# An attention block's backward stage: middle part reordered, side work given more yields and another step rate, dK stored from ScalarE one head later

## The chip, the cores and the metric

One core of one Trainium2 chip. The metric is device time in microseconds (us) of one launch. The kernel was already tuned: 1750 us in the median, with most runs within 0.4% of that. A ratio in this document is the mean time of one kernel's fast runs over that of the kernel before in the same rounds, with a 95% interval; so it is not quite the ratio of the two medians that stand beside it. "0.9942" means 0.58% faster, about 10 us; 0.1% is 1.75 us.

## The reference

A decoder block for one new token of each of 4 sequences: attention over a cache (32 heads, 4096 keys, head size 128), then a gated MLP, both after a layernorm, and the gradients of all inputs and weights.

```python
q = (layernorm(x) @ wq)                      # 4 x 32 heads x 128
p = softmax(q k^T / sqrt(128));  o = p v     # 4 x 32 heads over 4096 keys
h = x + o @ wo
out = h + (silu(lnh @ w1) * (lnh @ w3)) @ w2
out, vjp = jax.vjp(f, x, k_cache, v_cache, wq, wo, w1, w3, w2)   # out and 8 gradients
```

The caches make the weight of it: K and V are 128 heads of 1 MB each. The forward reads both; the backward stage reads V once more (dP = dO V^T) and writes dK and dV, 128 MB each. All else that is moved comes to 34 MB.

## The kernel before

All big tiles live in 22 buffers of 1 MB, handed out in a ring: a buffer that is given back goes to the end of the line, and who takes it next has to wait until the last transfer or instruction on it is over.

```python
free = deque(range(NSLOT))                 # 22 buffers
class Slot:
    def __init__(self, name): self.i = free.popleft(); ...
    def give(self):           free.append(self.i)
```

The backward stage goes head by head. `front` transposes V on TensorE (copies by ScalarE) and makes dP; `back` makes dV and dK as outer products on VectorE and stores both from GpSimd's queue. SyncE loads V up to seven heads ahead. Beside it runs a generator of "side work" (dq, dx and the weight gradients), cut by `yield` into about 200 steps, of which each head takes one, two or three.

```python
def grad_unit(dst, lhsT, rhs):             # one 128 x 512 piece of a weight gradient
    ...
    nc.tensor.matmul(ps[:, 0:n], lhsT=lhsT, rhs=rhs, start=True, stop=True)
    nc.scalar.copy(out=dst, in_=ps[:, 0:n])

def back(s):
    ...
    gv = Slot("gv"); outer(gv.heads(), P2, reps["rdo", s // REP][:, s % REP, :])
    nc.gpsimd.dma_start(out=rows_of(out_3[b, h]), in_=gv.heads()); gv.give()
    ...
    gk = Slot("gk"); outer(gk.heads(), dS2, reps["rq", s // REP][:, s % REP, :])
    nc.gpsimd.dma_start(out=rows_of(out_2[b, h]), in_=gk.heads()); gk.give()

def prefetch(s):
    while nv["next"] < min(NH, s + 7) and len(free) > 5:
        load_V2()                          # from SyncE

for s in range(NH):                        # NH = 128
    prefetch(s + 1)
    ...
    if s + 1 < NH: front(s + 1)
    back(s)
    step("s", 1 if s < 42 else 2 + s % 2)  # side work
step("s", 400)
```

Between forward and backward lies "the joint": the attention output times wo, the MLP and its backward for four rows, a serial chain whose weights hold most of the buffers.

## Time and profile before

The prediction below sizes the stages (the full forward, the joint, the full backward stage with a hole at 1160 us, the last stores) and shows the lines for it. Two views that it does not show are needed later. The first is the list of transfers by kind (count, KB each, median us from issue to landing); the second a table of windows of the second half (the last three columns: granted clock, DMA share, GB/s).

```profile
V<-in_A_v_cache_dram SPq DMA_DIRECT2D x128, 1024.0 KB, 11.1
out_dram<-gv POOLq DMA_DIRECT2D x128, 1024.0 KB, 19.6
out_dram<-gk POOLq DMA_DIRECT2D x128, 1024.0 KB, 19.6
```

### The profile page before, as it was taken

To read this page: it belongs to the slowest core of one execution; us is meant where nothing else is said; L and a number is where in the kernel's file an instruction comes from. 1 tells how busy PE (TensorE), PEld (TensorE's weight loads), DVE (VectorE), ACT (ScalarE), POOL (GpSimd) and SP (SyncE) were. 2 spreads that over 40 slices of the span, in tenths; PEclk is the share of its full clock that TensorE was granted. 3 is DMA by queue.
4 is the path that set the end of the run, shared out by engine and by line. 5 is a ranking of instruction groups with operands and counts; after the bars stand their busy time and mean duration, and the time that the engine had idled before them with its cause. 6 is when DMAs were issued, how large, how long until landed. Compare 5 with 4: busy or idle time off the path is not lost.

```text
span 1747.4 us, 44078 instructions
## 1 busy us (share of the span) xinstructions
PE 1324.0 (76%) x18993; PEld 1120.0 (64%) x18993; DVE 1254.4 (72%) x1385; ACT 953.7 (55%) x1460; POOL 487.4 (28%) x805
## 2 busy tenths in 40 slices
PE   5889888888888887878877886676787777476574
PEld 4667666677666666778766875555555556365563
DVE  5989899889998995557756757565465667475585
ACT  3455445445444544555554555675666667475463
POOL 2333333333333330112421333222222123132132
PEclk8999999999999999655555556765565556565555
DMA  9999999999999998699999999999999999999997
GB/s 398 410 418 418 419 418 419 418 412 418 418 415 398 418 407 313 257 422 421 410 414 418 415 416 413 422 383 426 417 418 416 414 412 406 422 407 410 424 417 303
DMA packets 107123, 707.86 MB, mean 405 GB/s; under 512 B 11232, under 2 KB 18920, under 8 KB 23984
## 3 DMA queue, kind: packets, MB, share of 16 engines
q1 hardware_dynamic: 67280, 422.68, 59.1%
q0 software_dynamic: 39648, 282.36, 39.2%
q8 instruction: 149, 2.44, 0.5%
q14 instruction: 46, 0.38, 0.1%
HBM read 422.58 MB, written 282.34 MB: 403 GB/s over the span
## 4 chain that ended last, share of the span: by engine, by line
DMA 38%; DVE 11%; issue 6%; PE 4%; ACT 3%; POOL 1%; DVEq 0%; POOLq 0%; ACTq 0%; SPq 0%
DMA out_dram<-gk 22%; DMA out_dram<-gv 12%; DVE gk L1053 4%; DVE gv L1053 4%; DMA V<-in_A_v_cache_dram 2%; ACT VT L740 2%; PE pt_tps L739 1%; DMA out_dram<-gw 1%; POOL P L1049 1%; DMA w<-in_B_w_dram 1%; DVE PK L421 1%; DVE dS L1071 0%; PE M_ps L436 0%; DVE dSt L1068 0%; PE o_ps L961 0%
## 5 line engine op out<-in xcount | busy, mean ns | idle before, releaser
L740 ACT COPY VT<-pt_tps 128x1024 bf16<-128x1024 bf16 x512 | 492.4, 1016 | 250.7 <-PE pt_tps L739 122.8
L739 PE MATMUL pt_tps<-ident_b,V 128*128 128x128 bf16 x4096 | 458.2, 296 | 147.0 <-ACT VT L740 147.0
L739 PEld LDWEIGHTS <-V 128*128 128x128 bf16 x4096 | 408.1, 140 | 211.6 <-issue 202.1
L1053 DVE TENSOR_TENSOR gv<-P,reps 128x4096 bf16<-128x4096 bf16 x128 | 292.9, 2288 | 234.0 <-DMA out_dram<-gk 141.1
L1053 DVE TENSOR_TENSOR gk<-dS,reps 128x4096 bf16<-128x4096 bf16 x128 | 293.4, 2292 | 67.0 <-DMA out_dram<-gv 29.7
L421 DVE TENSOR_TENSOR PK<-Kn,PK 128x4096 bf16<-128x4096 bf16 x128 | 302.9, 2366 | 35.9 <-POOL PK L417 35.9
L436 PE MATMUL M_ps<-PK,Vn 128*128 128x130 bf16 x4096 | 285.9, 222 | 47.0 <-DMA Vn<-in_A_v_cache_dram 46.1
L436 PEld LDWEIGHTS <-Vn 128*128 128x128 bf16 x4096 | 253.0, 99 | 67.3 <-DMA Vn<-in_A_v_cache_dram 61.0
L328 DVE STREAM_TRANSPOSE KT<-Kn 128x512 f32<-128x512 f32 (+1 forms) x321 | 250.9, 798 | 0.5 <-issue 0.5
L323 ACT COPY KT<-pt_tps 128x1024 bf16<-128x1024 bf16 x128 | 129.4, 1012 | 188.0 <-PE pt_tps L322 155.8
L1046 PE MATMUL dP_ps<-dOT_bf,VT 128*128 128x1 bf16 x4096 | 152.6, 166 | 66.0 <-ACT VT L740 65.3
L1046 PEld LDWEIGHTS <-VT 128*128 128x128 bf16 x4096 | 141.3, 104 | 78.1 <-ACT VT L740 77.6
L1075 POOL DMA_DIRECT2D out_dram<-gk x128 | 68.2, 533 | 384.3 <-DVE gk L1053 377.1
L1065 POOL DMA_DIRECT2D out_dram<-gv x128 | 68.4, 535 | 347.6 <-DVE dSt L1068 333.5
L417 POOL COPY PK<-P_all 128x64 bf16<-128x64 bf16 x128 | 32.3, 253 | 436.9 <-ACT P_all L411 424.6
L336 POOL COPY zq<-qT_bf 128x2 bf16<-128x2 bf16 x128 | 152.2, 1189 | 0.0
L1049 POOL COPY P<-P_all 128x64 bf16<-128x64 bf16 x128 | 117.4, 918 | 0.0
L411 ACT COPY P_all<-pt_P 32x64 bf16<-32x64 bf16 x256 | 51.9, 203 | 58.2 <-PE pt_P L407 56.0
L322 PE MATMUL pt_tps<-ident_b,Kn 128*128 128x128 bf16 x1024 | 80.6, 223 | 0.7 <-DVE qrep L282 0.7
L446 PE MATMUL kP_ps<-PK,onesw 128*32 128x512 bf16 x1024 | 79.2, 386 | 0.0
L322 PEld LDWEIGHTS <-Kn 128*128 128x128 bf16 x1024 | 62.1, 100 | 26.5 <-issue 26.5
L400 ACT ACTIVATE Pn<-E,rl 128x1024 bf16<-128x1024 f32 x64 | 73.7, 1151 | 2.8 <-DVE rl L397 2.8
(221 smaller groups left out, 1288.3 us busy)
## 6 DMA issues: line engine op xcount, KB each, us to landing
Kn<-in_A_k_cache_dram SPq DMA_DIRECT2D x128, 1024.0 KB, 14.9
Vn<-in_A_v_cache_dram SPq DMA_DIRECT2D x128, 1024.0 KB, 14.7
V<-in_A_v_cache_dram SPq DMA_DIRECT2D x128, 1024.0 KB, 11.1
out_dram<-gv POOLq DMA_DIRECT2D x128, 1024.0 KB, 19.6
out_dram<-gk POOLq DMA_DIRECT2D x128, 1024.0 KB, 19.6
wq<-in_A_wq_dram SPq DMA_DIRECT2D x8, 1024.0 KB, 14.6
out_dram<-gw POOLq DMA_DIRECT2D x6, 896.0 KB, 21.7
wo<-in_A_wo_dram SPq DMA_DIRECT2D x4, 1024.0 KB, 14.5
```

What stands on the lines that cost most here:

```text
L322: nc.tensor.transpose(pt[:, i, :], Kn[:, c * GW + i, :], ident_b[:])
L323: nc.scalar.copy(out=KT[:, c * GW:(c + 1) * GW, :], in_=pt[:])
L328: nc.vector.transpose(out=KT[:, c * w_:(c + n) * w_], in_=Kn[:, c * w_:(c + n) * w_])
L336: nc.gpsimd.tensor_copy(out=zq[gi % 2][hl][:, 32:132:67], in_=qT_bf[:, s:s + 1].to_broadcast([P, 2]))
L421: nc.vector.tensor_tensor(out=PK[:, :, 0:Dh].rearrange("p j (r t) -> p j r t", t=2), in0=Ks[s].heads().rearrange("p j (r t) -> p j r t", t=2),
L436: nc.tensor.matmul(hold["M"][:], lhsT=Vn[:, j, :], rhs=PK[:, j, :], start=(j == 0), stop=(j == SJ - 1))
L446: nc.tensor.matmul(hold["kP"][32 * q:32 * (q + 1), :, :], lhsT=ones_window(w), rhs=PK[:, j0:j0 + 4, 0:Dh], start=(w == 0 and c == 0), stop ...
L739: nc.tensor.transpose(pt[:, i, :], Vn[:, g * GW + i, :], ident_b[:])
L740: nc.scalar.copy(out=VT[:, g * GW:(g + 1) * GW, :], in_=pt[:])
L1046: nc.tensor.matmul(dP_ps[:, j:j + 1], lhsT=VT[:, j, :], rhs=dOT_bf[:, s:s + 1], start=True, stop=True)
L1049: nc.gpsimd.tensor_copy(out=P2[:], in_=P_all[:, s, :, None].to_broadcast([P, SJ, 2]))
L1053: nc.vector.tensor_tensor(out=dst.rearrange("p j (r t) -> p j r t", t=2), in0=col2[:, :, None, :].to_broadcast([P, SJ, Dh // 2, 2]), in1=r ...
```

## The change

Its intent: shorten the joint, so that buffers come free and V loads start sooner; take the waits out of the side work by more yields and by copying a gradient unit only when the next one is under way; take the dK stores off GpSimd's queue, so that three engines issue instead of two. No byte more or less moves. The core of the diff (the reordering of the joint, some 80 lines, is cut to two lines and a comment; the comments are ours):

```diff
+            # joint: w1/w3 transposes before the attention pages, wo transposes spread over the
+            # gaps, layernorm applied after the transposes, the first two V transposes no longer there
-        V_T(0, psT)
+        woT(5, "ssvsv")
...
         def grad_unit(dst, lhsT, rhs):
...
-            nc.scalar.copy(out=dst, in_=ps[:, 0:n])
+            grad_flush()                    # copy of the unit before
+            gu.append((dst, ps, n))
...
             wqT.give()
+            yield                           # eight yields more, this one ahead of dx's reader
             fs = Slot("fin")
...
             outer(gk.heads(), dS2, reps["rq", s // REP][:, s % REP, :])
-            nc.gpsimd.dma_start(out=rows_of(out_2[b, h]), in_=gk.heads())
+            late.append((b, h, gk))
+
+        def store_gk():
+            b, h, gk = late.popleft()
+            nc.scalar.dma_start(out=rows_of(out_2[b, h]), in_=gk.heads())
             gk.give()
...
                 front(s + 1)
+            if late:
+                store_gk()
             back(s)
-            step("s", 1 if s < 42 else 2 + s % 2)
+            step("s", 1 if s < 44 else 2 + (s % 4 == 0))
+        store_gk()
         step("s", 400)
```

More of the change, by code (lines that the diff above doesn't have):

```diff
@@ L476, in attn_page @@
         if pg == 0 or last:
-            hold["at"] = psX.tile([P, 512], FP32, tag="x", name="at_ps")
+            hold["at"] = psK.tile([P, 512], FP32, tag="kP", name="al_ps") if last else psX.tile([P, 512], FP32, tag="x", name="at_ps")
         at_ps = hold["at"]
         for k in range(8):
-            c = 0 if last else k % 4
+            c = 0 if last else k % 2
             nc.tensor.matmul(at_ps[32 * c:32 * c + B, :], lhsT=OT_bf[:, (8 * pg + k) * B:(8 * pg + k + 1) * B],
                              rhs=wo_page(8 * pg)[:, k].rearrange("p c n -> p (c n)"),
-                             start=(k == 0 if last else pg == 0 and k < 4), stop=(k == 7 if last else pg == H // 8 - 2 and k >= 4),
+                             start=(k == 0 if last else pg == 0 and k < 2), stop=(k == 7 if last else pg == H // 8 - 2 and k >= 6),
                              tile_position=(0, 32 * c))
         if pg >= H // 8 - 2:
-            for c in range(1 if last else 4):
+            for c in range(1 if last else 2):
                 nc.vector.tensor_tensor(out=hrows[:], in0=hrows[:], in1=at_ps[32 * c:32 * c + B, :], op=ALU.add)
@@ L578 @@
     pending = deque()
-    for nm, ap in (("w1", B_w1), ("w3", B_w3)):
+    for nm, ap in (("w3", B_w3), ("w1", B_w1)):
         for i in range(2):
@@ L693 @@
     weights(NGI)
-    w13T(4, "sv")
     M_mm(NH - 2, 0, SJ)
@@ L697 @@
     weights(NGI)
-    w13T(4, "sv")
     M_mm(NH - 1, 0, SJ)
@@ L702 @@
     O_cols(NH - MC, NH)
+    kP_flush(NH - 1)
     w13T(len(tunits), "sv")
-    kP_flush(NH - 1)
     for pg in range(H // 8 - 1):
         attn_page(pg)
-        woT(4, "sv")
+        if pg > 0:
+            woT(1, "s")
     attn_page(H // 8 - 1)
@@ L756 @@
         psT = cm.enter_context(tc.tile_pool(name="psTm2", bufs=4, space=bass.MemoryType.PSUM))
-        hs = Slot("hhat")
-        hhat = hs.f(D)[0:B, :]
         while free:
             load_V2()
-        layernorm_rows(hrows[:], B, hhat, rstd_h[:])
-        nc.scalar.activation(out=warm[:], in_=warm[:], func=AF.Exp)
-        woT(len(wo_units), "s")
+        pt = psA.tile([P, DC, B], FP32, tag="rT", name="pt_hT")
+        for c in range(DC):
+            nc.tensor.transpose(pt[:, c, :], hrows[0:B, c * P:(c + 1) * P], ident_f[0:B, 0:B])
@@ new lines @@
+        stats = small.tile([B, 1, nc.vector.BN_STATS_DIM], FP32, tag="ln_stats", name="ln_stats")
+        nc.vector.bn_stats(out=stats[:, 0, :], in_=hrows[:])
+        mv = small.tile([B, nc.vector.BN_AGGR_DIM], FP32, tag="ln_mv", name="ln_mv")
+        nc.vector.bn_aggr(out=mv[:], in_=stats[:])
+        nc.vector.tensor_scalar(out=rstd_h[:], in0=mv[:, 1:2], scalar1=eps, scalar2=None, op0=ALU.add)
+        woT(1, "s")
+        nc.scalar.sqrt(rstd_h[:], rstd_h[:])
+        nc.scalar.activation(out=warm[:], in_=warm[:], func=AF.Exp)
@@ new lines @@
+        woT(2, "s")
+        rdiag = mid.tile([B, 2 * B], FP32, name="rdiag")
+        nc.vector.tensor_scalar(out=rdiag[:, 0:B], in0=ident_f[0:B, 0:B], scalar1=mv[:, 0:1], scalar2=None, op0=ALU.mult)
+        nc.vector.reciprocal(out=rstd_h[:], in_=rstd_h[:])
+        nc.vector.tensor_scalar(out=rdiag[:, B:2 * B], in0=ident_f[0:B, 0:B], scalar1=rstd_h[:], scalar2=None, op0=ALU.mult)
+        rb_ps = psA.tile([P, 2 * B], FP32, tag="rT", name="rb_ps")
+        nc.tensor.matmul(rb_ps[:], lhsT=ones_f[0:B, :], rhs=rdiag[:], start=True, stop=True)
@@ L764 @@
+        woT(1, "s")
+        rb = mid.tile([P, 2 * B], FP32, name="rb")
+        nc.vector.tensor_copy(out=rb[:], in_=rb_ps[:])
         hhatT = mid.tile([P, DC, B], BF16, name="hhatT")
         hhatT_f = mid.tile([P, DC, B], FP32, name="hhatT_f")
-        pt = psA.tile([P, DC, B], FP32, tag="rT", name="pt_hT")
-        for c in range(DC):
-            nc.tensor.transpose(pt[:, c, :], hhat[:, c * P:(c + 1) * P], ident_f[0:B, 0:B])
-        nc.vector.tensor_copy(out=hhatT[:], in_=pt[:])
-        nc.vector.tensor_copy(out=hhatT_f[:], in_=pt[:])
@@ L771 @@
-        nc.gpsimd.tensor_copy(out=hhat_bf[:], in_=hhat)
-        hs.give()
-        while free:
-            load_V2()
+        nc.vector.tensor_tensor(out=hhatT_f[:], in0=pt[:], in1=rb[:, None, 0:B].to_broadcast([P, DC, B]), op=ALU.subtract)
+        nc.vector.tensor_tensor(out=hhatT[:], in0=hhatT_f[:], in1=rb[:, None, B:2 * B].to_broadcast([P, DC, B]), op=ALU.mult)
+        nc.vector.tensor_tensor(out=hhatT_f[:], in0=hhatT_f[:], in1=rb[:, None, B:2 * B].to_broadcast([P, DC, B]), op=ALU.mult)
@@ L775 @@
+        nc.vector.tensor_scalar(out=hhat_bf[:], in0=hrows[:], scalar1=mv[:, 0:1], scalar2=rstd_h[:],
+                                op0=ALU.subtract, op1=ALU.mult)
         w1, w3 = mid_w["w1"], mid_w["w3"]
@@ L783 @@
             sl.give()
-        while len(free) > 1:
+        while free:
             load_V2()
-        rdiag = mid.tile([B, B], FP32, name="rdiag")
-        nc.vector.tensor_scalar(out=rdiag[:], in0=ident_f[0:B, 0:B], scalar1=rstd_h[:], scalar2=None, op0=ALU.mult)
-        rb_ps = psA.tile([P, B], FP32, tag="rT", name="rb_ps")
-        nc.tensor.matmul(rb_ps[:], lhsT=ones_f[0:B, :], rhs=rdiag[:], start=True, stop=True)
-        rb = mid.tile([P, B], FP32, name="rb")
-        nc.vector.tensor_copy(out=rb[:], in_=rb_ps[:])
         gateT = mid.tile([P, FC, B], FP32, name="gateT")
@@ L821 @@
             sl.give()
-        while len(free) > 1:
+        while free:
             load_V2()
-        V_T(1, psT)
+        woT(len(wo_units), "s")
         z = mid.tile([P, 2, DC, B], FP32, name="z")
@@ L841 @@
                                        in1=u[:], op0=ALU.mult, op1=ALU.add)
-        nc.vector.tensor_tensor(out=u[:], in0=u[:], in1=rb[:, None, :].to_broadcast([P, DC, B]), op=ALU.mult)
+        nc.vector.tensor_tensor(out=u[:], in0=u[:], in1=rb[:, None, B:2 * B].to_broadcast([P, DC, B]), op=ALU.mult)
         nc.vector.tensor_tensor(out=dhT[:], in0=u[:], in1=grT[:], op=ALU.add)
@@ L876, with grad_flush @@
         bw3 = c2.enter_context(tc.tile_pool(name="bw3", bufs=3, reuse_waits="tile"))
+        gu = []
+        def grad_flush():
+            if gu:
+                dst, ps, n = gu.pop()
+                nc.scalar.copy(out=dst, in_=ps[:, 0:n])
         def grad_unit(dst, lhsT, rhs):
@@ L899, in side_work @@
             flat = Slot("dqflat")
+            yield
             for b in range(B):
@@ L928, in side_work @@
                             nc.tensor.transpose(pt[:, i, cc, :], wv[:, cc, (hl + i) * Dh:(hl + i + 1) * Dh], ident_b[:])
+                    yield
                     nc.scalar.copy(out=wqT.b(HH * D).rearrange("p (n c) -> p n c", c=P)[:, hl * DC:(hl + 2) * DC, :],
                                    in_=pt.rearrange("p a c k -> p (a c) k"))
-                    yield
                 wq2.give()
+                yield
                 for hl in range(HH):
@@ L938, in side_work @@
             wqT.give()
+            yield
             fs = Slot("fin")
@@ L954, in side_work @@
                     yield
+                grad_flush()
                 nc.gpsimd.dma_start(out=out_4[cc * P:(cc + 1) * P, :], in_=st.b(HD))
@@ L963, in side_work @@
                 sl.give()
+            yield
             h2_bf = rs.t[0:B, 2560:2560 + D]
@@ L974, in side_work @@
                         nc.tensor.transpose(pt[:, c, :], srcT[:, c0 + c, :], ident_b[:])
+                    yield
                     nc.scalar.copy(out=dst_rows[:, c0 * P:(c0 + 7) * P].rearrange("b (c f) -> b c f", f=P), in_=pt[:])
-                    yield
             for i in range(2):
@@ L982, in side_work @@
                     yield
+                grad_flush()
                 nc.gpsimd.dma_start(out=out_8[i * 7 * P:(i + 1) * 7 * P, :].rearrange("(c p) j -> p c j", p=P),
@@ L993, in side_work @@
                             yield
+                    grad_flush()
                     nc.gpsimd.dma_start(out=out_ap[i * 2 * P:(i + 1) * 2 * P, :].rearrange("(c p) f -> p c f", p=P),
@@ L1012, in side_work @@
                     yield
+                grad_flush()
                 nc.gpsimd.dma_start(out=out_5[h0 * P:(h0 + 8) * P, :].rearrange("(h p) j -> p h j", p=P),
@@ L1074, in back @@
             outer(gk.heads(), dS2, reps["rq", s // REP][:, s % REP, :])
-            nc.gpsimd.dma_start(out=rows_of(out_2[b, h]), in_=gk.heads())
+            late.append((b, h, gk))
+        late = deque()
+        def store_gk():
+            b, h, gk = late.popleft()
+            nc.scalar.dma_start(out=rows_of(out_2[b, h]), in_=gk.heads())
             gk.give()
```

## The prediction

> **What bounds the kernel now.** I read the page's slices first, then a table of windows by stage, then the chain of work that ended last between 690 and 730 us, and the longest waits.
>
> The first fence is the page's second part, 40 slices of 43.7 us each.
>
> ```profile
> PEclk8999999999999999655555556765565556565555
> DMA  9999999999999998699999999999999999999997
> GB/s 398 410 418 418 419 418 419 418 412 418 418 415 398 418 407 313 257 422 421 410 414 418 415 416 413 422 383 426 417 418 416 414 412 406 422 407 410 424 417 303
> ```
>
> The DMA row is full nearly everywhere: no engine sets the pace, the 16 transfer engines do. Only four places fall below: slices 15 and 16 (313, 257 GB/s), slice 26 (383) and the last (303). The page gives 422.58 MB read and 282.34 MB written, and the change moves no byte more or less; at the 424 GB/s that full 5 us windows reach, these 704.9 MB take 1663 us. So time can come only from the holes and from the rate in full stretches. The table of windows (columns: length, busy us and count of PE, PEld, DVE, ACT, POOL, then clock, DMA share, GB/s) sizes the stages:
>
> ```profile
> 0.00:660.00 660.00, 542.30 (x9045) 445.96 (x9045) 585.55 (x798) 319.74 (x705) 219.36 (x399) 0.98 1.01 414
> 660.00:740.00 80.00, 65.55 (x1123) 56.95 (x1123) 38.94 (x70) 39.20 (x60) 7.77 (x14) 0.77 0.75 273
> 740.00:1730.00 990.00, 716.11 (x8831) 617.12 (x8828) 629.86 (x519) 594.81 (x696) 260.22 (x392) 0.57 1.01 415
> 1730.00:1747.00 17.00, 0.00 (x0) 0.00 (x0) 0.00 (x0) 0.00 (x0) 0.00 (x0) 0.50 0.33 138
> ...
> 1160.00:1172.00 12.00, 8.28 (x125) 6.40 (x123) 10.36 (x15) 8.82 (x11) 0.53 (x1) 0.78 0.76 275
> ```
>
> The forward (to 660) and backward stages (740 to 1730) run at 414 and 415 GB/s. Against 420, the joint between them loses 80 x (1 - 273/420) = 28 us, the hole at 1160 loses 12 x (1 - 275/420) = 4.1 us, and the tail 17 x (1 - 138/420) = 11.4 us. These 44 us are all there is to win without a higher rate.
>
> Why the joint is a hole: its weights hold 20 of the 22 buffers with the M tiles, so V loads for the backward stage wait until weight buffers are given back, which the serial middle part does. Its chain (start, us, what):
>
> ```profile
> 700.55 0.59 DVE xr L487
> 701.15 0.02 issue
> 701.17 0.69 DVE xr L487
> 701.86 0.02 issue
> 701.88 0.69 DVE xr L487
> 702.58 0.02 issue
> 702.60 0.70 DVE xr L487
> 703.30 0.04 issue
> 703.34 1.90 PE at_ps L481 x8
> ...
> 708.75 3.05 PE gu_ps L780 x112
> 711.81 0.52 PE rb_ps L790 x2
> 712.32 3.53 PE pt_tps L739 x32
> 715.85 2.96 PE dn_ps L817 x112
> 718.81 3.44 PE pt_tps L739 x32
> ```
>
> The matmuls of gu free four buffers at 711.8, those of dn four more at 718.8. The hole at 1160 shows among the waits as a single one of VectorE, during which no gradient tile is made:
>
> ```profile
> DVE fin L941 <- PE dx_ps L935: 10.0, 1, 10.0
> ```
>
> **What the Trainium skill says.** "DMA: Bandwidth & Descriptors", section "Issuing engines are not separate DMA queues": DMAs from any issuing engine run on the same 16 engines and interleave; several issuers save only sequencer time. The trace agrees so far: the hardware queue's 422.68 MB take 59.1% of 16 engines' span, 409 GB/s, the software queue's 282.36 MB 39.2%, 412 GB/s. Moving dK to ScalarE's queue should therefore not raise the rate. The same page, section "Latency and other measured facts": engines 7 and 15 are usually slower, perhaps because of the rings of GpSimd's queue, which the hardware queue lacks. The trace shows a straggle that may be this: after the bulk ends at about 1733, the DMA share is 0.19 for 5 us and 0.07 for 5 more, about one engine of 16. It does not show which one. "SBUF — State Buffer", section "Who interferes with whom": a VectorE operation can starve GpSimd's descriptor writing. The trace shows no such loss: the store issues of dK on GpSimd take 532 ns at the least and 547 at the most, although GpSimd's own copies beside VectorE stretch from 0.25 to 1.48 us. "ScalarE: Activation LUTs", section "What ACT_TABLE_LOAD costs" gives 1283 ns a load; the trace has 1.28 us after the square root. The change keeps it there, beside other work.
>
> **The change part by part.**
>
> First, the path from the last forward head to gu. In the kernel before, transposes of w3 wait for their load (PE idle around 676 to 679) ahead of the last two heads' matmuls. The change runs those first, at about 677 and 679 (their last product is made by 676.8), then the kP flush, free at about 682 instead of 695; with it the first two V loads can go at about 682 to 684, so their 2 MB follow the weights without a gap. All 112 transposes of w1/w3 come next: eight ScalarE copies of 1.01 us set their time, 8.3 us, to about 690. Between the four attention pages there are then two wo units instead of twelve: 10 x 8 transposes at about 0.06 us is 4.9 us of PE removed. The hrows additions fall from five to three, 2 x 0.69 = 1.4 us, and the last page uses another PSUM buffer, so it no longer waits for the first additions. Pages and additions end at about 693.5, not 705.95. The new layernorm transposes raw rows and applies mean and rstd later, by a PE broadcast and two VectorE operations: some 0.6 us dearer than normalising first, and the square root can wait up to 1 us behind a wo copy on ScalarE. I put gu's start at 697.5 instead of 708.75: 11 us sooner.
>
> Second, from gu to the backward stage. Two V transposes (3.53 and 3.44 us) leave and ten wo units (80 transposes at the half clock, about 0.11 us each, 4.4 us for each five) come in their place. Before, each half carried four ScalarE copies of 1.02 us, now it carries up to five, so this part gets 1 to 2 us longer. dOT should end at 718 instead of 727.5 and the first dV tile start at 722 instead of 731.4: 9.5 us earlier.
>
> Third, the restart, which pays some back. The two V transposes are now owed there: PE per head takes about 6.5 us at half clock (734.56 to 741.27), so dK of head 0 is ready at about 730. Its store waits on ScalarE for the transposes of two heads later, to about 738. V loads are ten by then and stop at about 719, since the look-ahead is seven heads and five buffers stay in reserve. From 719 to 743 only about four 1 MB stores flow. Bytes from 660 to 744: before, 23.6 MB (summing 4 us windows); after, 10.7 MB by the end of the weights as before, plus ten V loads (10.5), plus about 4.3 of stores, 25.5 MB. The difference, 1.9 MB at 420 GB/s, is **4.5 us gained** in the joint, not 9.5.
>
> Fourth, the side work. A yield before the use of dx and between other matmuls and their readers removes the 10.0 us VectorE wait: **4 us gained** (the whole hole at 1160). Eight yields more in all (about 207 for 199) and a slower step rate end it at head 116 or so instead of 105, still before the end. Copies of gradient units, one unit late, spare ScalarE waits such as 17.7 us in 20 pieces: hidden, zero.
>
> Fifth, the queues. ScalarE gets 128 issues; an unhindered V load issue on SyncE took 0.33 us, so 42 us in all. ScalarE is busy 595 of 990 us in this stage: hidden. GpSimd loses 68.2 us of issues, zero on the path. Holding a dK tile one head longer costs one buffer, while a landing of 19.6 us at 7.8 us per head keeps five stores in flight: still saturated, zero. At the tail, half of the stores leave the software queue; I allow **3 us** of the 11.4.
>
> Sum: 4.5 + 4 + 3 = 11.5; 1750.6 - 11.5 = 1739. I lean a little lower, to **1737 us**, because small holes (828 to 836 and 1568 to 1576, 1.5 us each by their windows) may also shrink with looser waits.
>
> **The rivals.** (a) The queue change itself raises the rate: three queues share the engines, and mixed windows reach 421 to 429 GB/s while the store-only end runs at about 416. One per cent over 990 us is 10 us: 1727. Against it: equal rates of both queues above. (b) Stragglers are due to the software queue and half the tail goes: 1734. (c) ScalarE becomes a bound: it now waits for dK of the previous head before its V copies, and VT copies feed dP. If this coupling exposes 0.1 us per head it costs 13 us: 1750. For it: ScalarE already waits 63.6 us for stores of dV to free VT buffers; against it: a dK tile is a full head old when it is issued. (d) The restart with late dK stores and no loads in hand eats the whole joint gain: 1742.
>
> **Range and chances.** The range 1722 to 1748 spans (a) with the sum at the low end and (c) or (d) at the high end. Over 2% faster needs below 1716, 35 of the 44 us of holes or a rate gain with them: 0.05. Slower by over 2% needs 35 us of new stalls that nothing here shows: 0.01. Within 2%: 0.94.
>
> **What would show it.** gu near 697 to 699, the first dV near 722; a hole in GB/s at 693 to 699 and a second at 719 to 743; no long wait of VectorE for dx and no hole near 1160; 414 to 416 GB/s in the full backward stretch; dK issues on ScalarE with waits for dK on VectorE below 1 us each. I am wrong if the backward rate rises to 419 or more (rival a), if the joint still moves under 280 GB/s over its 80 us (d), or if ScalarE's copies wait in sum much longer with the DMA share below 1.0 (c).

## More of the kernel before

```profile
660.00:756.00 96.00, 78.46 (x1272) 69.07 (x1272) 47.52 (x75) 48.07 (x70) 9.85 (x19) 0.73 0.79 298
756.00:1000.00 244.00, 195.26 (x2366) 183.35 (x2366) 165.42 (x136) 136.06 (x148) 66.64 (x100) 0.54 1.01 417
1000.00:1250.00 250.00, 176.32 (x2183) 146.69 (x2182) 152.40 (x134) 151.59 (x177) 67.60 (x93) 0.62 1.00 412
1250.00:1500.00 250.00, 184.74 (x2160) 145.49 (x2158) 148.07 (x121) 165.51 (x211) 60.79 (x98) 0.57 1.01 414
1500.00:1730.00 230.00, 146.88 (x1978) 129.47 (x1976) 155.40 (x125) 132.76 (x153) 63.11 (x96) 0.57 1.01 416
```

A V load lands in 11 us, a store in 20. Every window after the joint runs at 412 to 417 GB/s: the transfers set the pace, and a stage can be judged by one number, its GB/s.

## The result, and the profile after

The changed kernel took 1748.39 us in the median (1746.43 to 1751.21, 4 runs) against 1750.12 (1749.51 to 1755.61, 4 runs): a ratio of 0.9984, interval 0.996 to 1.0009. About 2 us were gained where 11.5 to 13.5 had been predicted, and the time lies just above the range.

The joint's chain came out as predicted, and so did its two holes, 55 GB/s from 693 to 699 us and 227 from 719 to 743. Columns: start, us, what.

```profile
698.67 3.09 PE gu_ps L792 x112
...
714.00 3.40 PE dOT_ps L853 x128
```

gu starts at 698.67 (predicted 697.5, before 708.75); the first dV tile starts at 721.3 (predicted 722, before 731.4). Yet little of it is left. The slices of the page, 43.7 us each, and the windows of the second half:

```profile
GB/s 397 409 419 418 419 419 419 419 414 418 414 418 395 419 406 344 287 391 420 421 419 419 420 416 385 420 395 384 423 425 398 424 413 411 392 412 420 420 403 346
```

```profile
660.00:756.00 96.00, 82.52 (x1300) 71.45 (x1301) 51.69 (x78) 54.01 (x76) 14.73 (x19) 0.78 0.82 311
756.00:1000.00 244.00, 194.13 (x2369) 182.61 (x2367) 161.89 (x133) 135.31 (x148) 66.89 (x66) 0.54 1.01 420
1000.00:1250.00 250.00, 159.24 (x2104) 134.65 (x2101) 153.36 (x131) 138.49 (x157) 53.47 (x63) 0.64 0.99 403
1250.00:1500.00 250.00, 180.04 (x2183) 141.85 (x2183) 146.14 (x120) 165.50 (x209) 60.31 (x66) 0.60 1.01 413
1500.00:1730.00 230.00, 158.60 (x1998) 133.09 (x1997) 153.75 (x125) 143.97 (x173) 69.90 (x66) 0.56 1.00 413
```

Slices 15 and 16 rose from 313 and 257 to 344 and 287, but slice 17 fell from 422 to 391: the restart goes on with holes where the kernel before was already full. And where the kernel before had one hole in its backward stretch (383), this one has several (385, 395, 384, 398, 392). In the windows, a difference of GB/s times length, divided by 420 GB/s, is time: the joint gains 13 x 96 / 420 = 3.0 us, 756 to 1000 gains 1.7, 1000 to 1250 loses 9 x 250 / 420 = 5.4, the next loses 0.6, and 1500 to 1730 loses 1.6. The tail gains: in steps of 5 us over the last 30 us of each trace, the shortfall against 420 GB/s adds up to 12.0 us before and to 7.8 now.

Transfers and waits changed, too:

```profile
V<-in_A_v_cache_dram SPq DMA_DIRECT2D x128, 1024.0 KB, 17.2
out_dram<-gv POOLq DMA_DIRECT2D x128, 1024.0 KB, 19.1
out_dram<-gk ACTq DMA_DIRECT2D x128, 1024.0 KB, 12.8
```

```profile
ACT gwq L888 <- DMA V<-in_A_v_cache_dram: 18.4, 2, 16.8
ACT reps L1056 <- DMA V<-in_A_v_cache_dram: 14.9, 2, 10.5
...
DVE fin L959 <- PE dx_ps L952: 6.1, 1, 6.1
```

dK stores land in 12.8 us instead of 19.6, at the cost of the V loads, 17.2 instead of 11.1. The Trainium skill, "DMA: Bandwidth & Descriptors", section "Queues, rings and completion order", says that each transfer engine serves the queue rows that have work in turn, a packet at a time. The landings agree with it: two of three rows now store, where one of two did. The wait lines (us in sum, times, longest) show ScalarE waiting for V loads, 58 us in all such groups, although no instruction of ScalarE reads V; the kernel before has no such line. In the trace the transfers of SyncE's and ScalarE's queues use the same eight completion semaphores (the counters that tell of a landing), while GpSimd's have eight of their own; 54 of the 128 dK stores follow a V load on their semaphore, and before 53 of them ScalarE waits for it. That fits the lines; that this is the whole of their cause was not tested by itself. Nor did these waits lengthen ScalarE's idle time: from 740 to 1730 us it is busy 594.8 us before and 594.0 after, so they stand in place of other waits. VectorE's wait for dx went from 10.0 to 6.1 us, not to zero.

So three suspects stood against the gain of the joint: the queue, the late copies with their yields, and the step rate.

### The profile page after: what moved, and what is told of

Its sections match the earlier page's. It is cut to its first block, busy times and chain, and to the rows that moved or that the text cites. A ratio compares the mean times of both kernels' runs of the same rounds, so it can differ in the third digit from the quotient of the medians.

```text
span 1746.9 us, 43919 instructions
## 1 busy us (share of the span) xinstructions
PE 1315.9 (75%) x18993; PEld 1108.9 (63%) x18993; DVE 1252.2 (72%) x1381; ACT 956.9 (55%) x1464; POOL 484.7 (28%) x676
## 4 chain that ended last, share of the span: by engine, by line
DMA 32%; PE 11%; ACT 9%; DVE 5%; issue 4%; POOL 1%; ACTq 0%; DVEq 0%; POOLq 0%; SPq 0%
DMA out_dram<-gv 12%; ACT VT L739 8%; DMA out_dram<-gk 7%; DMA V<-in_A_v_cache_dram 6%; PE pt_tps L738 4%; DVE gv L1076 3%; DMA out_dram<-gw 2%; DMA out_dram<-gwo 2%; DMA wq<-in_A_wq_dram 2%; DMA out_dram<-gwq 1%; PE dq_ps L901 1%; PE dP_ps L1069 1%; DVE PK L421 1%; PE rep_ps L1053 1%; PE pt_wo L575 1%
## 5 line engine op out<-in xcount | busy, mean ns | idle before, releaser
L738 PE MATMUL pt_tps<-ident_b,V 128*128 128x128 bf16 x4096 | 449.3, 292 | 112.7 <-ACT VT L739 112.6
L738 PEld LDWEIGHTS <-V 128*128 128x128 bf16 x4096 | 398.4, 137 | 207.9 <-issue 199.0
L1076 DVE TENSOR_TENSOR gk<-dS,reps 128x4096 bf16<-128x4096 bf16 x128 | 293.9, 2296 | 69.1 <-DMA out_dram<-gk 31.7
L1072 POOL COPY P<-P_all 128x64 bf16<-128x64 bf16 x128 | 183.6, 1435 | 0.0
L1091 DVE TENSOR_SCALAR dSt<-dP_ps,c_rep 128x32 f32<-128x32 f32 x128 | 31.3, 245 | 97.1 <-PE dP_ps L1069 97.1
## 6 DMA issues: line engine op xcount, KB each, us to landing
V<-in_A_v_cache_dram SPq DMA_DIRECT2D x128, 1024.0 KB, 17.2
out_dram<-gk ACTq DMA_DIRECT2D x128, 1024.0 KB, 12.8
```

Of the source, the lines that this page charges most:

```text
L738: nc.tensor.transpose(pt[:, i, :], Vn[:, g * GW + i, :], ident_b[:])
L1072: nc.gpsimd.tensor_copy(out=P2[:], in_=P_all[:, s, :, None].to_broadcast([P, SJ, 2]))
L1076: nc.vector.tensor_tensor(out=dst.rearrange("p j (r t) -> p j r t", t=2), in0=col2[:, :, None, :].to_broadcast([P, SJ, Dh // 2, 2]), in1=r ...
```

## The experiments

Eighteen runs in five groups, all with correct results; those of one group ran on the same chip and share their runs of the kernel before. The table is by group; each is told below.

| group | kernel | median us (before) | ratio, 95% interval |
|---|---|---|---|
| 1 | changed, dK from GpSimd, one head late | 1745.26 (1751.21) | 0.9970, 0.9942 to 0.9998 |
| 1 | changed, dK from GpSimd at once | 1748.04 | 0.9978, 0.9960 to 0.9997 |
| 1 | before + dK from ScalarE late, only | 1751.42 | 0.9997, 0.9976 to 1.0018 |
| 1 | before + the joint, only | 1745.52 | 0.9956, 0.9934 to 0.9979 |
| 2 | changed, look-ahead of 4 | 1755.59 (1751.12) | 1.0025, 1.0010 to 1.0041 |
| 2 | the same with dK from GpSimd late | 1744.55 | 0.9961, 0.9949 to 0.9973 |
| 2 | joint + yields around dx | 1740.96 | 0.9942, 0.9930 to 0.9954 |
| 2 | joint + ScalarE stores for the last ten heads | 1742.88 | 0.9957, 0.9945 to 0.9969 |
| 3 | changed, dK from GpSimd at once, old rate | 1743.33 (1752.61) | 0.9949, 0.9931 to 0.9968 |
| 3 | joint + yields around dx, new rate | 1746.02 | 0.9979, 0.9952 to 1.0006 |
| 3 | changed, dK from GpSimd at once (repeat) | 1748.35 | 0.9974, 0.9950 to 0.9998 |
| 3 | joint + yields around dx (repeat) | 1741.10 | 0.9937, 0.9918 to 0.9955 |
| 4 | joint + yields around dx + dK from ScalarE late | 1745.34 (1753.22) | 0.9954, 0.9937 to 0.9972 |
| 4 | changed, old rate | 1744.28 | 0.9948, 0.9931 to 0.9965 |
| 4 | joint + yields around dx, three steps a head | 1749.00 | 0.9972, 0.9954 to 0.9989 |
| 4 | joint + yields around dx + dK from GpSimd late | 1741.66 | 0.9931, 0.9913 to 0.9949 |
| 5 | joint + yields around dx, alternation reversed | 1751.20 (1751.88) | 0.9987, 0.9966 to 1.0008 |
| 5 | joint + yields around dx, started two heads later | 1742.26 | 0.9943, 0.9929 to 0.9957 |

### First group: the parts alone

Undo the engine, and keep the lateness:

```diff
-            nc.scalar.dma_start(out=rows_of(out_2[b, h]), in_=gk.heads())   # in store_gk
+            nc.gpsimd.dma_start(out=rows_of(out_2[b, h]), in_=gk.heads())
```

> The changed kernel with one thing put back: dK is stored from GpSimd's queue again, still one head late. Theory Q (the hardware queue is the cost: ScalarE's stores and SyncE's loads share eight completion semaphores, so each waits for the other's earlier transfers, and in-order ScalarE and SyncE stand still): the backward stage from 740 to 1730 us returns from 411 to 415 GB/s or more, waits of ScalarE for V loads (58 us in the changed kernel) go to near zero, and the time falls by 6 to 10 us against the changed kernel, to 0.993 to 0.996 of the kernel before. Rival L (holding a dK tile one head longer starves the buffers): no change, 0.998 to 1.000. Rival S (the rescheduled side work makes the holes): no change either.

Measured: 0.9970, between the range of theory Q and that of its rivals. V loads land in 11.3 us again, no wait of ScalarE for V is left, and the joint (660 to 756) runs at 333 GB/s instead of 311.

Undo the whole store part, so that the joint and the side work of the change remain:

```diff
-            late.append((b, h, gk))
+            nc.gpsimd.dma_start(out=rows_of(out_2[b, h]), in_=gk.heads())
+            gk.give()
...
-        store_gk()
```

> The changed kernel with its store part undone altogether: dK from GpSimd as soon as it is made. What stays is the joint and the side work. Theory Q: as e1, 0.993 to 0.996 of the kernel before. Rival L: only now does the loss go, so 0.993 to 0.996 here and 0.998 to 1.000 in e1. Rival S: 0.998 to 1.000 in both.

Measured: 0.9978, just outside the range of rival S and well outside that of Q. Without any ScalarE store most of the expected gain is still missing, so the queue is not the main loss.

The store part alone, in the kernel before (the diff's last two hunks but for the rate):

> The kernel before with nothing but the store part of the change: dK from ScalarE's queue one head late. Theory Q and rival L: slower than the kernel before by 4 to 10 us (1.002 to 1.006), the backward stage at about 411 to 413 GB/s, less some 3 us gained at the tail. Rival S: no slower, 0.996 to 1.000.

Measured: 0.9997. Nothing gained, nothing lost in sum. Its trace has the waits of ScalarE for V (72.6 us), 422 GB/s from 756 to 1000 (417 before), 402 from 1000 to 1250 (412 before), and a tail short by 8.2 us instead of 12.0: gains and losses of the queue cancel here.

The joint alone: the changed text up to the backward stage, from there on the text before.

> The joint of the change alone (w3 first, transposes of wo spread, layernorm by broadcast, no V transposes there), the backward stage's code as before. By the bytes moved until 756 us the joint is worth about 3 us: 0.997 to 0.999 of the kernel before, the hole near 1160 still there. If the side work is a gain by itself (my step four, 4 us), e2 is some 4 us faster than this run; rival S says this run is as fast as e2 or faster.

Measured: 0.9956, better than expected, with 331 GB/s from 660 to 756; the hole near 1160 is still there. The window is worth (331 - 298) x 96 / 420 = 7.5 us, of which the next one (413 against 417 GB/s) gives back 2.3. In time, 0.44% of 1750 is 7.7 us (interval 3.7 to 11.6); a near-repeat in the second group, which differs in the last ten heads alone, gave 0.9957. The whole change is slower than its first part.

### Second group: look-ahead, dx, tail

If ScalarE's stores wait for V loads by shared semaphores, fewer loads in flight might free them:

```diff
-            while nv["next"] < min(NH, s + 7) and len(free) > 5:
+            while nv["next"] < min(NH, s + 4) and len(free) > 5:
```

> The changed kernel with the look-ahead of the V loads cut from seven heads to four, nothing else. With four, the V load whose completion semaphore a dK store takes over (about eight hardware-queue transfers or four heads earlier in the program) is one whose transposes ScalarE has already copied, so it has landed. Theory Q by shared semaphores: ScalarE's waits on V loads fall from 58 us to under 15, and the time falls by 3 to 6 us against the changed kernel (0.994 to 0.997 of the kernel before). Rival A (three queue rows in rotation give loads too small a share): loads then have less lead, so the time rises or stays, 0.998 or more. If the stores' own place in ScalarE's order costs most, no change either.

Measured: 1.0025. That idea fell: ScalarE's waits for V stayed at 63.7 us, V loads landed in 21.6 us, and TensorE now waited for V itself (27.1 us). The same edit with dK from GpSimd:

> Control of the run with look-ahead four: the same cut in the version whose dK is stored late from GpSimd, where no store shares a semaphore with a load. Theory Q: nothing to free, so equal to or up to 4 us slower than with look-ahead seven (0.996 to 1.000 of the kernel before). If it gains as much as the ScalarE version, the look-ahead helps for another reason and Q by shared semaphores is not supported.

Measured: 0.9961, no loss from the shorter look-ahead although TensorE waited 44.1 us for V. With little in hand, the queue of the dK stores makes 0.6%, the largest effect of it that we saw.

The joint with only those yields that stand around dq, the wq transposes and dx:

```diff
+            yield
             t = rs.f(2080)[:, 1536:1536 + NH]
...
             flat = Slot("dqflat")
+            yield
...
+                    yield
                     nc.scalar.copy(out=wqT.b(HH * D)...)
-                    yield
                 wq2.give()
+                yield
...
             wqT.give()
+            yield
```

> The joint, plus of the side work only the yields around dq, the wq transposes, dx and the final layernorm; gradient units, their late copies and the step rate as before. If step four's mechanism was right and only the rest of the side work (one-late copies, slower rate, side work spread to head 116) costs, the dx hole near 1160 goes and the time is 2 to 4 us below the joint alone, 0.990 to 0.995 of the kernel before. If any rescheduling of side work only moves the hole, it is equal to the joint alone or slower, 0.995 to 0.998.

Measured: 0.9942, 0.14% (2.4 us) below the joint alone, and 1.9 us below the joint with other last ten heads; single runs overlap in both. In the trace VectorE no longer waits for dx at all. But the hole did not go. It only stands a little later:

```profile
1176.00:1188.00 12.00, 8.81 (x107) 7.08 (x106) 7.36 (x7) 8.92 (x11) 2.54 (x3) 0.50 0.88 318
1188.00:1200.00 12.00, 9.60 (x96) 6.98 (x96) 11.71 (x10) 8.24 (x12) 4.87 (x8) 0.50 1.01 401
```

That is a shortfall of 3.5 us, where the hole of the kernel before was 4.1. So the wait for dx was not all that made the hole. Another thing stands still there in both kernels. SyncE also stores dx, and waits for it (`reps` holds it) with the next V loads behind it in its program. In the kernel before:

```profile
SPq L945 <- DVE reps L944: 31.7, 1, 31.7
```

With the yields it is 32.2 us. No run moved this store, so its part in the hole is not shown.

This version is better than the changed kernel by 7 us; what it lacks of it are the store part, the late copies with a few yields, and the new rate.

The joint with late ScalarE stores in the last ten heads only, to have the shorter tail without the rest:

> The joint, plus dK from ScalarE's queue one head late for the last ten heads only, when few or no V loads are left to share semaphores with. The drain after the last store issue is 19 to 20 us with GpSimd alone, and some 12 of them are lost bandwidth against 8 in the changed kernel. If that is the hardware queue's doing, this run keeps the gain of 3 to 4 us: 0.992 to 0.994 of the kernel before, 3 us below the joint alone. If the shorter drain came from elsewhere, it equals the joint alone.

Measured: 0.9957, the joint's own value. The expected gain did not come: its tail is short by 11.7 us, as before. The shorter tail of the changed kernel needs the stores on ScalarE all along, not only at the end.

### Third group: late copies or rate?

Two by two, with both corners repeated. The rate is one line:

```diff
-            step("s", 1 if s < 44 else 2 + (s % 4 == 0))     # as changed
+            step("s", 1 if s < 42 else 2 + s % 2)            # as before
```

All of the changed side work with the old rate:

> The changed kernel with dK stored at once from GpSimd (so the joint and all of its side work, late copies of gradient units and all yields), but with the step rate of the kernel before. Theory 1, the slower rate costs: side work holds its staging and operand buffers to about head 116 instead of 105, so fewer buffers are left for V loads and stores over more of the stage; then this run recovers most of what the side work lost: 0.994 to 0.996 of the kernel before. Theory 2, the late copies cost: a gradient unit's PSUM copy waits for the next unit, the staging buffer is full one unit later and ScalarE's copies come bunched; then this run stays near 0.998. Theory 3, neither: what we took for a loss was scatter between calls of 0.2%; then this run equals the repeats of both neighbours in this call within their intervals.

The yields around dx with the new rate:

> The joint and the yields around dx on the kernel before, immediate copies of gradient units, immediate stores from GpSimd, but with the changed kernel's step rate. Theory 1 (slow rate costs): 0.997 to 0.999 of the kernel before, 3 to 6 us above the same kernel with the old rate. Theory 2 (late copies cost): equal to the same kernel with the old rate within 0.1%, so 0.994 to 0.995.

The two corners again:

> A repeat, within this call, of the changed kernel with dK stored at once from GpSimd (0.9978 in the earlier call). If the side work's loss is real, 0.997 to 0.999; if it was scatter, 0.994 to 0.996.

> A repeat, within this call, of the joint with the yields around dx only (0.9942 in the earlier call). 0.993 to 0.995 if it is the better version; 0.996 or more if the earlier run was a lucky one.

Measured: with the old rate 1743.33 and 1741.10 us, with the new rate 1748.35 and 1746.02. The line costs 5.0 us beside late copies and 4.9 us beside immediate ones. Each pair by itself is hardly clear of its scatter; the twelve runs with the old rate and the twelve with the new differ by 5.2 us in the mean (95% interval 1.5 to 8.8). The late copies and the other yields make 2.2 and 2.3 us, inside the intervals. All four fall where the theory of the rate put them, and the earlier values repeat (0.9978 and 0.9974; 0.9942 and 0.9937). With the new rate the runs also scatter more: 1740.68 to 1755.91 against 1739.09 to 1745.94. The profiled run of the new-rate kernel with immediate copies was the fastest of its six, so its trace does not show the loss, and we do not read one from it.

### Fourth group: the change itself, the queue on the best base, and a higher rate

The changed kernel with nothing but the old rate:

> The changed kernel with nothing but the old step rate. If the slower rate is the term that failed, this recovers 4 to 6 us: 0.994 to 0.997. If with ScalarE's stores another thing sets the time, it stays at 0.998 or above.

Measured: 1744.28 us, 0.9948, as expected. Against the changed kernel's 0.9984 (each against its own runs of the kernel before) that is 0.36%, 6 us. One line of the change had cost this.

Its neighbours tell the queue. Late dK stores from ScalarE, and from GpSimd, each on the joint with the yields around dx:

> The best version so far (joint and yields around dx, old step rate, 0.994) plus only the store part of the change: dK stored from ScalarE one head later. Theory 1 (the shared row of loads and dK stores costs): 0.9955 to 0.998 of the kernel before, and ScalarE waits for V loads that it doesn't read, 50 us or more in sum. Theory 2 (the queue is neutral; what the earlier runs showed was scatter): 0.993 to 0.995. Theory 3 (the prediction's own: the tail gains 3 us): 0.991 to 0.993.

> As the run with dK from ScalarE one head later on the best version, but dK from GpSimd one head later. Lateness alone costs nothing by the prediction and by one earlier pair (0.997 against 0.998): 0.993 to 0.995. If lateness itself costs, by the buffer that it holds: 0.9955 or more, no better than ScalarE's.

Measured: 1745.34 against 1741.66 us. The six runs of one (1744.01 to 1749.54) lie above the six of the other (1740.68 to 1742.90) without overlap. Lateness costs nothing (0.9931 against 0.9937 for stores at once); the engine costs 4 us. The 0.9954 lies at the edge of theory 1, and ScalarE's waits for V are 45.5 us in sum, somewhat under the 50 it named. Where is the loss? At two places. The first is the restart. The first lines are from ScalarE's kernel, the second from GpSimd's: the issue of the first dK store, and the windows of 730 to 750 us.

```profile
737.91 0.38 ACTq L1090 DMA_DIRECT2D out_dram<-gk  x1
...
730.00:740.00 10.00, 8.72 (x116) 8.27 (x115) 7.19 (x6) 5.81 (x7) 2.61 (x2) 0.50 0.39 159
740.00:750.00 10.00, 8.59 (x93) 8.12 (x94) 7.85 (x8) 5.20 (x7) 5.19 (x4) 0.50 0.95 363
```

```profile
730.05 0.55 POOL L1090 DMA_DIRECT2D out_dram<-gk  x1 [5.38 <-DVE gk L1062]
...
730.00:740.00 10.00, 8.72 (x115) 8.33 (x114) 7.72 (x8) 5.05 (x6) 3.98 (x5) 0.50 0.87 288
740.00:750.00 10.00, 8.46 (x93) 7.82 (x91) 7.19 (x5) 5.98 (x8) 5.98 (x6) 0.50 1.00 410
```

The store stands at the same place in both programs, "one head late". GpSimd has little else to do and issues it as soon as VectorE has made dK (it waited 5.38 us for it). ScalarE reaches it only after the V copies of head 2, two heads on, 7.9 us later, and this when nearly nothing else is in flight. With the window from 750 to 760 (381 against 419) the shortfall is (129 + 47 + 38) x 10 / 420 = 5.1 us.

The second place is in the full stretch. The side work transposes wq there, and TensorE waits for the first load of it; again ScalarE's kernel comes first.

```profile
PE pt_wq L935 <- DMA wq<-in_A_wq_dram: 20.3, 1, 20.3
...
1068.00:1080.00 12.00, 0.00 (x0) 0.00 (x0) 0.00 (x0) 0.00 (x0) 0.78 (x2) 0.50 1.01 405
...
1092.00:1104.00 12.00, 9.51 (x139) 7.41 (x138) 7.41 (x6) 10.12 (x11) 1.55 (x4) 0.89 0.73 269
```

```profile
PE pt_wq L935 <- DMA wq<-in_A_wq_dram: 1.1, 1, 1.1
...
1092.00:1104.00 12.00, 8.60 (x127) 7.84 (x124) 10.68 (x9) 9.00 (x10) 4.76 (x6) 0.64 1.02 418
```

With ScalarE, SyncE issues this load at 1058.8 us and its reader starts at 1082.9; with GpSimd the two are 1043.7 and 1061.6. Meanwhile the engines stand still, and when what is in flight has landed, the rate falls. From 1056 to 1116 us the shortfall against the other kernel is 6.9 us. All five kernels with dK on ScalarE throughout have this wait, 16.0 to 24.3 us long; in the others no single one exceeds 7.6 us. Why the load goes out later was not followed further.

In the same two traces, later windows differ both ways: 421 against 417 GB/s from 756 to 1000, 407 against 418 and 408 against 413 in the next two, 421 against 406 in the last. The tail is short by 10.7 against 13.7 us.

Three steps a head on the best base, to test why the rate matters. We had read it as buffers: side work that ends sooner gives its buffers back sooner.

```diff
-            step("s", 1 if s < 42 else 2 + s % 2)
+            step("s", 1 if s < 42 else 3)
```

> The best version so far with a higher step rate: three steps of side work a head from head 42 on instead of 2.5, so that the side work ends some 10 heads sooner. If side work loses by the buffers that it holds and for how long, this is at or a little below the base: 0.991 to 0.994. If 2.5 was already the balance between that and the crowding of PE and ScalarE, it is equal or up to 0.3% slower: 0.994 to 0.997.

Measured: 0.9972, slower by 0.3% again. The reading "it holds buffers for longer" fell.

### Fifth group: average or placing

The same average of 2.5 steps with only the pieces moved, by reversing the alternation (`3 - s % 2`) or by starting two heads later (`s < 44`):

> The best base (joint and yields around dx, 0.994) with the same average step rate of 2.5 a head, but the alternation the other way round: three steps in even heads, two in odd ones. If the average is what matters: 0.993 to 0.995. If it is how the pieces fall beside single heads: it may be anything from 0.993 to 0.998, and 0.996 or more settles for that.

> The best base with only the first number of the change's rate: one step a head until head 44 instead of 42, then 2.5 on average as before, so all later side work comes about one head later. Same reading: 0.993 to 0.995 if the average rate matters, 0.996 or more if the placing of single pieces does.

Measured: 0.9987 for the first, 0.9943 for the second. The average is not what matters: with it unchanged, the reversed alternation kept only 0.13% of the 0.6% that the best base gains. It is the placing of single pieces of side work beside the heads. Of our kernels, the three patterns that put three steps into some even heads (the change's, three everywhere, the reversed one) are slow, and the two that put them into odd heads alone are fast; three against two is a hint, not a proof.

One place in the traces of the reversed and the unreversed kernel shows how a piece can make a hole. First the reversed one: windows, and VectorE's dV tile with the idle time before it.

```profile
1272.00:1284.00 12.00, 7.28 (x75) 5.53 (x75) 0.00 (x0) 7.44 (x10) 0.48 (x2) 0.50 1.01 425
1284.00:1296.00 12.00, 9.19 (x133) 6.62 (x132) 9.95 (x9) 7.56 (x9) 4.46 (x5) 0.93 0.79 321
...
1285.05 2.29 DVE L1062 TENSOR_TENSOR gv<-P,reps 128x4096 bf16<-128x4096 bf16 x1 [13.64 <-DMA out_dram<-gwq]
```

The same stretch with the alternation of the kernel before (the repeat of the third group):

```profile
1272.00:1284.00 12.00, 10.32 (x93) 6.33 (x91) 4.97 (x4) 6.59 (x9) 0.53 (x1) 0.64 1.01 421
1284.00:1296.00 12.00, 9.72 (x138) 7.87 (x136) 8.78 (x9) 9.01 (x11) 4.36 (x7) 0.83 1.01 408
...
1278.84 2.29 DVE L1062 TENSOR_TENSOR gv<-P,reps 128x4096 bf16<-128x4096 bf16 x1 [8.95 <-DMA out_dram<-gwq]
```

In both, the ring hands VectorE a buffer whose gradient store (gwq, issued at 1260.5 and 1260.7) has not landed. In one the store is over 18 us after its issue, in the other 25 us; VectorE makes no tile for 8.95 or for 13.64 us. The first is bridged by the stores in flight (421 and 408 GB/s), the second is not (321, then 362). The shortfall against the other, (408 - 321) x 12 / 420 plus (413 - 362) x 12 / 420, is 3.9 of the 6.8 us that separate the two profiled runs. Another 1.7 us (415 against 418 GB/s from 756 to 1000) had been lost before head 42, where the two programs are still the same: scatter. This is one place in one pair of traces. Why the pieces fall well in one pattern and badly in another stays open. A rival was not tested: the side work's own small transfers on SyncE, behind which V loads wait (in the kernel before 31.7 us for dx, 25.8 for the rows of the attention output).

## Why the prediction was right or wrong

- **The path to gu, and from gu to the backward stage: right.** 698.67 for 697.5, and 721.3 for 722.
- **The restart, 4.5 us gained: right within 1.5 us.** The changed kernel's windows give 3.0. The prediction had already deducted here what the late dK store costs ("waits on ScalarE ... to about 738"; measured 736.6). What it did not ask is what an engine that gets there at once would give: the joint alone, with dK on GpSimd, has 7.5 us in this window. Rival (d), that all of the joint's gain is eaten, did not come.
- **The side work's rate, "a slower step rate end it at head 116 or so instead of 105, still before the end": here the prediction failed.** It ends at head 116, but the rate was not free: it cost 4.9, 5.0 and 6 us in three pairs. The prediction asked only whether side work ends before the stage does. It left out that the pieces take buffers, engines and queues from the full stretch on the way, and that moving pieces alone moves the time by 9 us (1751.20 against 1742.26). No rival named it. Which of these makes the loss is open. The late copies were called hidden, and are, within the 2 us that the runs resolve: with ScalarE's stores and the old rate the change's full side work is at 0.9948, the dx yields alone at 0.9954.
- **The yields, "removes the 10.0 us VectorE wait: 4 us gained (the whole hole at 1160)": half wrong.** In the changed kernel 6.1 us of the wait stayed. Where it went altogether, the hole stayed, later and smaller by 0.6 us by its windows; in time some 2 us were gained, hardly beyond the scatter. The prediction had read the hole as "a single" wait of VectorE; SyncE's 31.7 us stood in the same stretch.
- **The queues, "hidden, zero", and the tail, 3 us: the tail right, the zero wrong.** The shortfall at the end fell by 4.2 us. But the prediction took the engine's busy share, 595 of 990 us, for its answer. With dK on ScalarE's queue the window from 1000 to 1250 lost 5.4 us in the changed kernel and 6.0 with the store part alone, and each such kernel has the long wait of TensorE for wq. Rival (c) named ScalarE's copies as the bound; new waits came (58 us for V loads, and some for dK itself, up to 8.3 us where the prediction said below 1), but its idle time did not grow. In total the queue cost 4 us on the best base, 0.14% within scatter in the changed kernel, nothing alone, nothing beside the full side work at the old rate (0.9948 against 0.9949), and 0.6% with a short look-ahead; nowhere did it gain. How much of the loss is shared semaphores and how much the loads' slower landing is open.
- **Rival (a), a higher rate by three queues: half seen, not in sum.** 420 to 422 GB/s against 417 from 756 to 1000, and 402 to 407 against 412 to 418 from 1000 to 1250.
- **The lean to 1737 for small holes:** unfounded. The change made new holes instead.

The sum with measured terms: the joint 7.7 us, dx 2.4, rate -6, queue with its tail 0 to -4, late copies 0 to -2 give 4 us gained to 2 lost; 2 to 3 were. With the rate line undone, the change gains 0.52%, about 9 us of the 11.5 that the prediction summed. That it comes so near is partly luck: the joint gave more than its term, the yields and the queue less.

The best version is the joint, the yields around dx, the old rate and dK from GpSimd one head later: 1741.66 us, 0.9931 (0.9913 to 0.9949), faster than both kernels.

## What to carry to other kernels

In a stage that transfers fill, the rate and the order at which background work is let in are not hidden because it ends in time: vary its placing by one step and time it before believing a gain or a loss of half a per cent. A wait that goes is not yet a hole that goes: look what else stands still in the same stretch, the engine that issues the loads above all. Before moving a store to another engine's queue, look up at which place of that engine's program it lands and what runs ahead of it, above all where few transfers are in flight; a mean busy share says nothing about it. And when a bundle of edits moves the time little, time its first part alone: here it was faster than the whole.

## What the Trainium skill lacked or had wrong

- "DMA: Bandwidth & Descriptors", section "Issuing engines are not separate DMA queues", says that several issuers only save sequencer time. The rate agrees on the whole (402 to 422 GB/s by window after the restart, with two issuers or three, but for 388 with the short look-ahead), but the choice is not neutral: with dK on ScalarE's queue, V loads landed in 17.2 us instead of 11.1 and dK stores in 12.8 instead of 19.6, and the first store went out at 737.91 instead of 730.05 us, since ScalarE issues it only when its program gets there.
- The same page, section "Queues, rings and completion order", explains the shift of the landings by taking turns between rows. It does not say that moving a store to a further row slows the loads of another; these landings show the shift, not its cause.
- No page that we found tells that a compiled program can put the transfers of two hardware queues on the same completion semaphores, so that one engine waits for the other's: here ScalarE waited 58 us for V loads that it does not read, and not at all with dK on GpSimd.
